# Moving LayerNorm's row factor from the matmul input to the residual add, and reordering the first batch, in a fused attention and MLP kernel

**Chip and metric.** One core of one Trainium2 chip. The metric is device time in microseconds (us). The time before is 672.65 us (median of three runs, 672.63 to 672.81). Spans below are the first to the last instruction of one profiled execution, some 2 us shorter than the device time.

## The reference

Eight batches; attention with normalized queries and keys, then LayerNorm and an MLP with a residual. Cut to what matters:

```python
# q, k, v: (8, 12, 448, 64) float32
q_n, k_n = rmsnorm(q, g_q), rmsnorm(k, g_k)
attn = softmax(q_n @ k_n^T / 8)
x = (attn @ v) -> (8, 448, 768)
mu, var = mean(x), mean((x - mu) ** 2)           # per row
xn = (x - mu) / sqrt(var + 1e-6) * g_ln
out = x + relu(xn @ w_ch1) @ w_ch2               # 768 -> 3072 -> 768
```

The row factor rs = 1/sqrt(var + eps) is positive, so relu(rs * a) = rs * relu(a): it can be left out of `xn` and applied to the row of the MLP's result. This identity is what the change uses.

## The kernel before

TensorE (PE) does all matmuls and transposes. Twelve heads make six pairs a batch; one pair has seven scores (matmul and exponential) and seven value steps. While the MLP of batch b runs on PE, the scores and values of batch b + 1 are slipped between its chunks. Batch 0 has nothing to hide behind, so its attention runs alone at the start. A batch has three row tiles of 128 (384 tokens); every second batch has a fourth tile, made of the leftover 64 tokens of two batches. The parts that matter, cut:

```python
def load_unit(self, u):                 # a unit: one or two pairs; K, Q, V
    ...
    for n, src in ((1, self.k), (0, self.q), (2, self.v)):
        eng.dma_start(<384 rows>)
        for e in range(2):
            eng.dma_start(<64 leftover rows>)

# PSUM accumulators of the values: one pair of buffers for all pairs
c["oA"] = self.ps_o.tile([128, 3, 130], FP32, tag="oA")
c["oB"] = self.ps_o.tile([128, 130], FP32, tag="oB")

def root():                                        # LayerNorm of a batch
    for t in range(n):
        nc.vector.bn_aggr(out=mv[:, t], in_=st[:, t, 0:18])
    _rsqrt(nc, c["rs"], mv[:, 0:n, 1], ...)        # exponential on ACT, 7 DVE ops
    nc.vector.scalar_tensor_tensor(out=c["sh"], ...)         # -mean * rs
def norm(t):
    nc.scalar.activation(out=t32, in_=tiles[t], func=AFT.Identity,
                         scale=c["rs"][:, t:t + 1], bias=c["sh"][:, t:t + 1])
    nc.vector.tensor_tensor(out=c["xn", t], in0=t32, in1=sh.gln, op=ALU.mult)

def down(t, g, s):                                 # second MLP matmul
    ...
    nc.vector.tensor_tensor(out=x[:, ts(g, 384)], in0=ps[:, 0:384],
                            in1=x[:, ts(g, 384)], op=ALU.add)

def run(self):
    ...
    frac = 0.77           # the next batch's attention ends at 77% of the MLP
    upto(int(min(goal, start + (goal - start) * done / total / frac)))
```

PE, ACT, GpSimd (POOL) and the load queue (SP) run in program order; VectorE (DVE) is ordered by a scheduler.

## Time and profile before

| | us |
|---|---|
| device time | 672.65 |
| span of the profile | 670.2 |
| first MLP matmul | 67.09 |
| from one batch's first MLP matmul to the next's | 77.38, 83.20, 69.83, 83.20, 70.12, 83.21, 66.33 |
| from the last batch's to the end | 69.84 |

Add the last two rows to 67.09 and the span is there. Batches 1, 3, 5 and 7 have four row tiles, so the rows of 83.2 and 69.8 differ by their MLP's size. The first LayerNorm in the timeline of the kernel before (start, length, engine, line, operation; at the end how long the engine had been idle, and for whom):

```profile
59.02 0.16 DVE L393 SCALAR_TENSOR_TENSOR sh<-stat,rs 128x3 f32<-128x3 f32 x1
59.21 1.95 ACT L399 ACTIVATE t<-x,sh,rs 128x768 f32<-128x768 f32 x2 [1.42 <-DVE sh L393]
60.27 1.88 DVE L401 TENSOR_TENSOR xn<-t,gln 128x768 f16<-128x768 f32 x2 [1.09 <-ACT t L399]
61.29 1.74 PE L421 MATMUL psX<-id,xn 128*128 128x128 f16 x12 [6.62 <-DVE xn L401]
...
67.09 0.80 PE L436 MATMUL psH<-xnT,w 128*128 128x384 f16 x2 [1.18 <-DVE xnT L423]
```

The values ended at 54.67 us (the prediction's 54.57 is the end of the last oA matmuls, a tenth before the last oB); PE then idles 6.6 us for the first normalized tile and starts the MLP 12.4 us after the values. The second view is PE alone in a four-tile batch, with attention slipped between the MLP's chunks:

```profile
158.08 0.54 PE L220 MATMUL psS<-qT,kT 128*128 128x448 f16 x2
...
158.71 1.46 PE L436 MATMUL psH<-xnT,w 128*128 128x512 f16 x6
...
160.29 0.35 PE L220 MATMUL psS<-qT,kT 128*128 128x448 f16 x1
```

Two scores stand back to back at 158.08: a "doubled step", where the spread of 0.77 puts two attention steps behind one MLP chunk. From the first of the six MLP matmuls behind it, 158.71, to the next score, 160.29, there are 1.58 us, where six such matmuls take 1.29: PE stood still for 0.29 us.

### The profile page before, as it was taken

Reading aid. Unit: us, or ns where it says so; the run is one execution under the profiler, and the core shown is the slowest. Engines: PE = TensorE matmul, PEld = TensorE weight load, DVE = VectorE, ACT = ScalarE, POOL = GpSimd, SP = SyncE. Lnnn points to the kernel's source line nnn. Section 1 sums busy time; section 2 is a strip of 40 time slices with the busy share of each in tenths; the row PEclk is TensorE's granted clock in tenths of the full one; section 3 lists DMA queues with packets and bytes.
Section 4 is the critical chain, followed back from the end, with each engine's and each line's share of the span. In section 5 each row is a group of like instructions: output and inputs, shape, how many; then the busy total and the mean of one; then the engine's idle time right before and its main releaser. Section 6 shows DMA issues by size and latency. Waiting matters only on the chain.

```text
span 670.2 us, 12546 instructions
## 1 busy us (share of the span) xinstructions
PE 620.5 (93%) x5066; PEld 379.5 (57%) x5066; DVE 373.8 (56%) x886; ACT 384.3 (57%) x669; POOL 91.6 (14%) x115
## 2 busy tenths in 40 slices
PE   1683899999999999999999999999999999999995
PEld 1352566655566666655566666655556666654463
DVE  4867667865556466765466466774465653380010
ACT  3884687647853487647763388637764287324300
POOL 2622222201220112202220022202201020000000
PEclk9995999999999999999999999999999999999999
DMA  5999973132131342122221242203331000010011
GB/s 147 219 220 220 215 184 82 54 108 77 52 84 47 93 113 66 51 66 67 82 83 48 60 122 59 80 24 107 83 84 47 28 22 1 25 48 1 0 48 51
DMA packets 72016, 54.81 MB, mean 82 GB/s; under 512 B 22928, under 2 KB 65936, under 8 KB 71952
## 3 DMA queue, kind: packets, MB, share of 16 engines
q1 hardware_dynamic: 62704, 44.22, 23.2%
q0 software_dynamic: 8528, 9.44, 8.2%
q8 instruction: 41, 0.67, 0.4%
q10 hardware_dynamic: 720, 0.30, 0.2%
q14 instruction: 23, 0.19, 0.1%
HBM read 52.36 MB, written 11.01 MB: 95 GB/s over the span
## 4 chain that ended last, share of the span: by engine, by line
PE 79%; DVE 10%; ACT 5%; issue 2%; SPq 1%; DMA 1%; POOL 0%; DVEq 0%
PE psH L436 30%; PE psC L447 27%; PE psS L220 7%; PE oA L246 4%; PE tr L202 2%; PE tr L189 2%; ACT E L227 2%; ACT khl L155 2%; PE oB L248 2%; DVE xn L401 1%; PE psS L223 1%; PE psS L224 1%; PE psX L421 1%; DVE stat L374 1%; ACT t L399 1%
## 5 line engine op out<-in xcount | busy, mean ns | idle before, releaser
L436 PE MATMUL psH<-xnT,w 128*128 128x512 f16 (+1 forms) x1152 | 246.6, 354 | 1.5 <-DVE xnT L423 1.5
L227 ACT ACTIVATE E<-psS,rr_all 128x448 f16<-128x448 f32 x336 | 208.4, 633 | 67.8 <-PE psS L220 51.4
L447 PE MATMUL psC<-w,hT 128*128 128x384 f16 x1344 | 239.3, 326 | 0.0
L438 ACT ACTIVATE hT<-psH 128x384 f16<-128x384 f32 (+1 forms) x192 | 104.6, 545 | 119.4 <-PE psH L436 117.5
L447 PEld LDWEIGHTS <-hT 128*128 128x128 f16 x1344 | 125.4, 98 | 72.4
L436 PEld LDWEIGHTS <-w 128*128 128x128 f16 x1152 | 105.6, 98 | 84.0 <-issue 4.0
L220 PE MATMUL psS<-qT,kT 128*128 128x448 f16 x288 | 101.7, 360 | 9.8 <-ACT E L227 7.5
L150 POOL TENSOR_TENSOR t<-t,gprod 128x896 f32<-128x896 f32 x22 | 45.8, 2082 | 427.2 <-issue 199.6
L246 PEld LDWEIGHTS <-E 128*128 128x128 f16 x1008 | 72.7, 99 | 54.2 <-issue 6.6
L246 PE MATMUL oA<-v,E 128*128 128x65 f16 x864 | 68.6, 195 | 1.5 <-DVE x L263 1.5
L451 DVE TENSOR_TENSOR x<-psC,x 128x384 f32<-128x384 f32 x48 | 26.7, 555 | 60.6 <-PE psC L447 60.2
L191 DVE COPY kT<-tr 128x960 f16<-128x960 f16 x48 | 31.5, 655 | 40.1 <-PE tr L189 39.6
L248 PE MATMUL oB<-v,E 128*128 128x65 f16 x288 | 52.9, 195 | 0.2
L261 DVE RECIPROCAL rec_all<-oA 128x6 f32<-128x6 f32 x48 | 9.4, 196 | 73.8 <-PE oA L246 73.8
L207 DVE COPY qT<-tr 128x896 f16<-128x896 f16 x45 | 28.0, 622 | 29.9 <-PE tr L202 29.6
L220 PEld LDWEIGHTS <-kT 128*128 128x128 f16 x288 | 28.5, 100 | 22.5 <-issue 3.3
L158 DVE TENSOR_TENSOR khl<-t,khl 128x896 f16<-128x896 f32 x22 | 24.0, 1091 | 18.0 <-ACT khl L155 17.8
L248 PEld LDWEIGHTS <-E 128*128 128x128 f16 x336 | 32.8, 98 | 0.9 <-DVE xl L268 0.5
L144 DVE TENSOR_REDUCE ssq<-qn 128x14 f32<-128x896 f32 (+1 forms) x25 | 26.2, 1046 | 10.1 <-ACT qn L141 9.1
L401 DVE TENSOR_TENSOR xn<-t,gln 128x768 f16<-128x768 f32 x28 | 26.9, 968 | 8.8 <-ACT t L399 8.8
L144 DVE TENSOR_REDUCE ssq<-khl 128x14 f32<-128x896 f32 (+1 forms) x25 | 26.2, 1047 | 10.0 <-ACT khl L141 9.4
L399 ACT ACTIVATE t<-x,sh,rs 128x768 f32<-128x768 f32 x24 | 23.8, 1021 | 13.0 <-DVE sh L393 12.3
(83 smaller groups left out, 536.7 us busy)
## 6 DMA issues: line engine op xcount, KB each, us to landing
out_dram<-x SPq DMA_DIRECT2D x24, 384.0 KB, 2.3
t<-in_k_dram SPq DMA_DIRECT2D x22, 384.0 KB, 3.5
t<-in_q_dram SPq DMA_DIRECT2D x22, 384.0 KB, 4.1
t<-in_v_dram SPq DMA_DIRECT2D x22, 384.0 KB, 4.3
w<-in_moe_w_ch_dram POOLq DMA_DIRECT2D x3, 1536.0 KB, 24.1
w<-in_moe_w_ch_dram POOLq DMA_DIRECT2D x2, 2304.0 KB, 44.1
out_dram<-xl SPq DMA_DIRECT2D x8, 192.0 KB, 3.1
t<-in_k_dram SPq DMA_DIRECT2D x44, 32.0 KB, 3.5
```

What stands on the lines that cost most here:

```text
L144: nc.vector.tensor_reduce(out=c["ssq"][:, n], in_=c["sq", n], axis=AX.X, op=ALU.add)
L150: nc.gpsimd.tensor_tensor(out=c["t"][:, 1], in0=c["t"][:, 1], in1=sh.gprod.unsqueeze(1).broadcast_to([128, g, D]), op=ALU.mult)
L191: nc.vector.tensor_copy(out=kT.rearrange("p g d -> p (g d)"), in_=ps[:, 0:960])
L220: nc.tensor.matmul(ps[:, 0:S], kT[:, 192 + 128 * i:320 + 128 * i], qT[:, h * S:(h + 1) * S], start=True, stop=True)
L227: nc.scalar.activation(out=c["E"][:, i], in_=ps[:, 0:S], func=AFT.Exp, scale=self.rr[:, 1, g:g + 1], bias=EXP_BIAS)
L246: nc.tensor.matmul(oA[:, t, cs], E[:, i, ts(t, 128)], rhs, start=(i == 0 and t == 0), stop=(i == 6 and t == 2))
L248: nc.tensor.matmul(oB[:, cs], E[:, i, 320:448], rhs, start=(i == 0), stop=(i == 6))
L399: nc.scalar.activation(out=t32, in_=tiles[t], func=AFT.Identity, scale=c["rs"][:, t:t + 1], bias=c["sh"][:, t:t + 1])
L401: nc.vector.tensor_tensor(out=c["xn", t], in0=t32, in1=sh.gln, op=ALU.mult)
L436: nc.tensor.matmul(ps[:, 0:N], sh.w1[:, dc, ts(f, 128)], xnT[:, dc, 0:N], start=(dc == 0), stop=(dc == NDC - 1))
L438: nc.scalar.activation(out=hT[:, f, 0:N], in_=ps[:, 0:N], func=AFT.Relu)
L447: nc.tensor.matmul(ps[:, 0:384], hT[:, f, ts(t, 128)], sh.w2[:, f, ts(g, 384)], start=(f == 0), stop=(f == NFF - 1))
```

## The change

Its intent: (1) leave rs out of the normalized tile, so that LayerNorm needs one DVE pass per tile instead of an ACT and a DVE pass, and no root ahead of it; (2) load the first batch tensor by tensor and order its preparation by hand; (3) a second pair of value accumulators in batch 0, in the MLP's PSUM buffers, which are idle then; (4) spread the attention over the MLP until ten chunks of 0.96 us before its end, instead of 77%. XS = 32 is multiplied into LayerNorm's weight and taken out again in the row factor. The core of the diff (cut: loads, checks of rs's range, small preparation ops):

```diff
+FIRST_ORDER = [      # (step, unit, operations of that unit's preparation)
+    (-2, 0, "begin", "sq", "sk", "kg", "tq", "rootq", "tk", "khi", "qn", "qdup", "klo", "rootk"),
+    (-2, 1, "begin", "sk", "sq", "kg", "tk", "tq", "khi"),
+    (-1, 1, "root", "klo", "qn", "qdup"),
+    ...
+]
+XS = 32.0
@@ loads of batch 0
+        for eng, n in ((nc.sync, 0), (nc.scalar, 1)):    # Q, K
+            main(eng, n, 0)                              # pair 0
+            left(eng, n)                                 # leftovers of all 12 heads
+        main(nc.scalar, 1, 1)
+        ...
+            nc.sync.dma_start(sh.gln, ...)
+            nc.vector.tensor_scalar(out=sh.gln, in0=sh.gln, scalar1=XS, ...)
@@ values
+            if p in (1, 3, 5):
+                c["oA"] = self.ps_m.tile([128, 3, 130], FP32, tag="mlp", name="oA")
+                c["oB"] = self.ps_m.tile([128, 130], FP32, tag="mlp", name="oB")
@@ LayerNorm
-            nc.scalar.activation(out=t32, in_=tiles[t], func=AFT.Identity,
-                                 scale=c["rs"][:, t:t + 1], bias=c["sh"][:, t:t + 1])
-            nc.vector.tensor_tensor(out=c["xn", t], in0=t32, in1=sh.gln, op=ALU.mult)
+            nc.vector.scalar_tensor_tensor(out=c["xn", t], in0=tiles[t], scalar=mv[:, t, 0:1],
+                                           in1=sh.gln, op0=ALU.subtract, op1=ALU.mult)
         def first():
+            aggregate()
+            for t in range(3):
+                norm(t)
             root()
-            norm(0)
-            norm(1)
@@ copies of the transposes, first batch
+        if b == 0 and t < 2:
+            nc.scalar.copy(out=self.xnT[:, :, ts(t, 128)], in_=ps)
@@ residual
-                nc.vector.tensor_tensor(out=x[...], in0=ps[:, 0:384], in1=x[...], op=ALU.add)
+                nc.vector.scalar_tensor_tensor(
+                    out=x[...], in0=ps[:, 0:384], scalar=self.rs[:, b, t:t + 1],
+                    in1=x[...], op0=ALU.mult, op1=ALU.add)
@@ run
-            upto(self.pos + 2)
-        frac = 0.77
+            upto(self.pos + 1)
+        tail = 10
-                upto(int(min(goal, start + (goal - start) * done / total / frac)))
+                upto(int(min(goal, start + (goal - start) * done / (total - 960 * tail))))
```

## The prediction

> **What bounds the kernel now.** I read the page's totals and slices first, then the chain of waits, then who TensorE (PE) waited for, stretch by stretch.
>
> ```profile
> span 670.2 us, 12546 instructions
> PE 620.5 (93%) x5066; PEld 379.5 (57%) x5066; DVE 373.8 (56%) x886; ACT 384.3 (57%) x669; POOL 91.6 (14%) x115
> PE   1683899999999999999999999999999999999995
> PE 79%; DVE 10%; ACT 5%; issue 2%; SPq 1%; DMA 1%; POOL 0%; DVEq 0%
> ```
>
> PE is full from about the fifth of 40 slices (16.8 us each) to the last. A busy PE need not be at its peak, so I checked the rate in the chain in order of time:
>
> ```profile
> 67.09 4.39 PE psH L436 x18
> ...
> 144.63 1.29 PE psH L436 x6
> ...
> 297.66 1.29 PE psH L436 x6
> ...
> 631.83 31.21 PE psC L447 x192
> ```
>
> Six matmuls of 512 columns take 1.29 us, 215 ns each; 192 of 384 columns take 31.21 us, 163 ns each. Two batches take 297.66 - 144.63 = 153.0 us; the next two pairs of batches, read the same way, 153.3 and 153.5. So from the first MLP at 67.09 to the last matmul at 663.04 the kernel is 596 us of PE work with little air, and the change takes no matmul away: both compiled kernels have 11,915 instructions on PE, in the listings of each engine’s order that can be had without running them; the order of the changed one is read there too. What is left to win is before 67.09 and in the idle time between. In a table of stretches (columns: length, then PE, weight loads, DVE, ACT and POOL busy us with counts, granted clock, DMA share, GB/s):
>
> ```profile
> 0.00:15.00 15.00, 2.33 (x16) 1.69 (x17) 6.22 (x23) 4.76 (x9) 3.25 (x11) 1.00 0.54 141
> 15.00:30.00 15.00, 9.24 (x66) 5.25 (x64) 12.69 (x27) 11.65 (x21) 10.12 (x14) 1.00 0.87 216
> 30.00:45.00 15.00, 10.85 (x133) 7.22 (x133) 11.06 (x29) 13.67 (x24) 6.61 (x7) 1.00 1.12 220
> 45.00:60.00 15.00, 7.62 (x92) 4.93 (x88) 8.68 (x31) 7.25 (x13) 0.00 (x0) 0.76 1.16 220
> 60.00:67.00 7.00, 2.46 (x18) 1.78 (x19) 6.70 (x10) 4.93 (x7) 4.10 (x4) 0.50 1.25 219
> 67.00:109.00 42.00, 39.93 (x343) 25.41 (x343) 28.89 (x63) 32.88 (x63) 10.19 (x12) 0.97 0.89 180
> ```
>
> PE is busy for 32.5 of the first 67 us. From 15 to 30 DVE is the fullest, from 30 to about 52 ACT (13.67 of 15), then comes a serial stretch of LayerNorm. PE's waits, whole run and first 67 us:
>
> ```profile
> PE psX L421 <- DVE xn L401: 10.7, 6, 6.6
> PE tr L186 <- DVE khl L158: 10.1, 1, 10.1
> PE psS L220 <- ACT E L227: 7.5, 17, 2.1
> ...
> PE psX L421 <- DVE xn L401: 8.7, 2, 6.6
> ```
>
> Of the 10.7 us that PE waited for the normalized tile, 8.7 lie in the first LayerNorm and only 2.0 at all later ones, 0.5 at a time. That is the size of what the LayerNorm part can give later.
>
> **What the skill says.** "TensorE: Matmul & The Clock Gate", section "Back-to-back issue gap": N/2.4 + 2.5 ns between matmuls when warm, N/1.2 when cold. The trace agrees: 215 ns at 512 warm, 0.32 us between the first matmuls of 384 at 67.09, 0.163 later. Its section "What's actually happening" says that about 3.4 us of activity release the clock; here the weight loads after 67.09 keep the cold spacing until 69.61. "VectorE: DVE Perf Modes", section "The perf-mode tier table": an fp32 tensor_tensor runs one element a cycle and cannot go faster. It has no row for the fused three-operand form; the trace has both on 128x896 at 1091 ns (tensor_tensor) and 1092 ns (fused), so I price fused as tensor_tensor. "DMA: Bandwidth & Descriptors", section "Specifications", gives 512 B as the least transfer for line rate; the leftover rows go in pieces of 256 B, and the change puts those of all 12 heads first. No row of this trace isolates that.
>
> **The change, part by part, in the first stage.**
>
> *Start.* Before, issue was slow: SP needs about 0.6 us an issue, 9 issues a unit, and the batch's last load went out at 22 us. After, Q and K of pair 0 come with the leftovers of all heads (six times the pieces), so I put their landing at 7.2 instead of 5.97 (K). From there I walked the changed order of each engine by hand with durations of the trace: square 0.58, reduce 0.62, small DVE operation 0.2, K product on POOL 1.13, low half 0.62, copy of K transposed 0.65, qn 0.63. K's transposes start at 10.7 (before 10.12). But DVE's new order puts the reductions of pair 1 ahead of pair 0's last root step and qn, so qn ends at 14.2, its duplicate (now on DVE) at 14.8, the transposes at 15.9, the copy of qT at 16.7, and the first exponential starts at 17.2 (before 16.84). Nothing is won here; pair 1 and the squares of the third unit are further along.
>
> *Pair 0 to pair 1.* ACT has two exponentials done at 18.3, then its order wants the root of unit 2, whose DVE work ends at 20.6. Three more exponentials, then the copy of pair 1's qT, which needs qn of pair 1, and that stands in DVE's queue behind the scaling of the LayerNorm weight, which needs a load issued behind the whole batch (about 23 us at the 220 GB/s that the table shows). That gives seven exponentials done at 27.3; before, nine were done at 26.98.
>
> *The ACT-bound stretch.* In the old kernel, 33 exponentials from 26.98 at 0.61 us, plus squares and high half of unit 3 (3 x 0.95), a root (0.22) and two qT copies (2 x 0.91), make 25.0 and end at 52.0; the trace has 51.99, so the sum is a fair model. After: 35 exponentials at 0.59 (second pair of accumulators), 2 x 0.95 since the high half moves to POOL, 0.22 and 1.82, from 27.3: 51.9. So the move of three high halves (0.57 + 2 x 0.95 = 2.5 us of ACT) and the earlier squares are eaten by the slower start.
>
> *Last pair.* In the old kernel PE waited 1.03 us for the accumulator of pair 4 to be read, then ran all of pair 5's value matmuls: 2.6 us from last exponential to the end. With accumulators in the MLP's PSUM for pairs 1, 3 and 5 they keep up: 0.4 us, ending at 52.3 instead of 54.57.
>
> *First LayerNorm.* Before: 67.09 - 54.57 = 12.5 us (evacuation, statistics, aggregate 2.8; root 1.85; two passes per tile on ACT and DVE; third tile behind squares of the next batch). After, from the end of the values: aggregate done at 2.8, three fused passes of 0.94 end at 5.6, with no root ahead of them; then ACT has the root's exponential (6.0), a square of 0.95 (7.0) and two copies of transposes at about 0.8: 8.55. Saved 3.95. So the first MLP matmul moves from 67.1 to 52.3 + 8.55 = 60.9: 6.2 us.
>
> *Later.* ACT loses 28 passes of 1.02 us and DVE keeps 28 passes of the same length (0.97); neither bounds. The residual add, 0.555 us, becomes a fused form of equal price. What goes is the 2.0 us of waits at the boundaries: first tile ready about 4.3 us after the last accumulator instead of 7.5. The shorter tail (ten chunks of 0.96 us instead of 10.6 and 14.1 us) still covers that. The root is needed only by the first residual, tens of us later.
>
> *Sum.* 6.2 + 2.0 = 8.2. My walk charged every stall that DVE's order permits and kept the whole cold start of the MLP (8 matmuls at 0.32 instead of 0.163, 1.25 us); I take 1.2 us of that back as likely too harsh. 672.65 - 9.4 = 663.2.
>
> **Rivals.** (1) The start is better than my walk: pair 0's scores at 12 to 13 us because Q and K land at 6 and DVE does not wait for pair 1. For: the author ordered this by hand, surely for that; ACT has spare time before 25 us. Against: DVE's printed order. It would add up to 4 us: 657 to 660, and some of it is over 2%. (2) Transfers take over: the table shows 216 to 220 GB/s without a break to about 90 us, the first 15 us at 141. An MLP that starts 6 us earlier wants its weights and the next batch earlier. For: the queue was full. Against: all of the batch goes out sooner, the second MLP weight had landed at 92 and was first used at 108.5. If it bites, 2 to 4 us come back: 666. (3) PE's own work is the limit and the later stages give nothing, or the denser spread of the attention makes ACT late: 665 to 667. (4) DVE gets longer queues at the boundaries (three passes in a row) and delays K and Q copies of the next pairs: 0.5 us each, 3 in all.
>
> **Range and chances.** The front is uncertain by 3.5 us either way, the later stages by 2, so 656.5 to 668.5. Over 2% means under 659.2, a win of 13.5 us of the 34.6 that PE idled in the first 67: 0.22. Slower by over 2% has no mechanism I can find, 0.02. Within 2%: 0.76.
>
> **What would show it.** First MLP matmul near 60.9 (58 to 63.5); first exponential near 17; ACT the fullest from 27 to 52; end of the values to first MLP matmul 8.5 us; no wait of PE on the normalized tile after the first batch; 153 us for two batches unchanged; the last 31 us unchanged. I would be wrong if the two-batch time moves by over 1 us, if the first exponential comes before 14.5, or if PE waits for weights after the first MLP starts.

## The result, and the profile after

662.25 us (median of four runs, 661.82 to 662.91) against 672.64 us (four runs, 672.23 to 672.81). The ratio is 0.9847, 95% interval 0.983 to 0.9864: 1.5% less, in the class "same" at the 2% line. The span of the profile went from 670.2 to 660.8 us.

From the page of the changed kernel: span, totals, and the chain of waits by engine.

```profile
span 660.8 us, 12501 instructions
PE 618.4 (94%) x5066; PEld 380.7 (58%) x5066; DVE 377.6 (57%) x890; ACT 358.4 (54%) x641; POOL 92.5 (14%) x113
PE 83%; DVE 8%; ACT 4%; DMA 2%; issue 1%; SPq 1%; ACTq 0%; DVEq 0%
```

ACT lost 26 us of work, DVE gained 4, PE kept its 5066 matmuls. Nearly all of ACT's 26 us was beside PE's work, as the small gain says. The chain in order of time, about the first MLP matmul of batches 0, 1 and 3:

```profile
61.08 7.28 PE psH L523 x30
...
138.00 1.29 PE psH L523 x6
...
290.07 1.29 PE psH L523 x6
```

The rate of the matmuls is the same (1.29 us for six), the first MLP starts 6.01 us earlier, and two batches take 290.07 - 138.00 = 152.07 us instead of 153.03. The table of stretches of the changed kernel (length, then PE, weight loads, DVE, ACT and POOL busy us with counts, granted clock, DMA share, GB/s):

```profile
0.00:15.00 15.00, 0.93 (x7) 0.66 (x7) 8.87 (x32) 4.24 (x10) 3.52 (x9) 1.00 0.80 226
15.00:30.00 15.00, 9.31 (x54) 5.25 (x55) 11.82 (x28) 10.24 (x17) 10.86 (x11) 1.00 0.96 243
30.00:45.00 15.00, 12.39 (x155) 8.78 (x154) 12.36 (x31) 12.98 (x24) 7.13 (x10) 1.00 1.12 213
45.00:60.00 15.00, 8.93 (x110) 6.04 (x106) 10.45 (x30) 8.38 (x15) 0.22 (x1) 0.85 1.21 221
```

The first 15 us move 226 GB/s instead of 141, yet PE does less there (0.93 us instead of 2.33): the earlier data does not reach PE. ACT remains the fullest between 30 and 45. PE's waits over the whole run (who waited for whom: us in total, times, longest):

```profile
PE tr L262 <- DVE khl L218: 11.3, 1, 11.3
PE psS L296 <- ACT E L302: 5.7, 11, 2.3
...
PE psX L505 <- DVE xn L479: 4.0, 1, 4.0
...
PE psC L534 <- DVE x L538: 1.9, 4, 0.5
```

The wait for the normalized tile is 4.0 us, all of it in the first LayerNorm; before it was 10.7, six times. A new one is the last line: four times 0.5 us, PE waits for a residual add to free an MLP buffer. There is no wait for weights. The first LayerNorm in the timeline:

```profile
55.62 2.81 DVE L479 SCALAR_TENSOR_TENSOR xn<-x,stat,gln 128x768 f16<-128x768 f32 x3
56.63 2.68 PE L505 MATMUL psX<-id,xn 128*128 128x128 f16 x18 [4.04 <-DVE xn L479]
58.69 0.95 ACT L198 ACTIVATE khl<-qkv 128x896 f32<-128x896 f32 x1
59.55 1.48 ACT L508 COPY xnT<-psX 128x768 f16<-128x768 f16 x2
59.78 2.07 POOL L207 TENSOR_TENSOR qkv<-qkv,gprod 128x896 f32<-128x896 f32 x1 [16.83 <-issue]
59.82 2.05 DVE L59 SCALAR_TENSOR_TENSOR stat<-stat 128x3 f32<-128x3 f32 x1
61.08 1.44 PE L523 MATMUL psH<-xnT,w 128*128 128x384 f16 x4 [1.77 <-ACT xnT L508]
```

Three fused passes, the transposes behind each, a square for the next batch, two copies, the MLP. From the end of the values (52.59) to the MLP there are 8.49 us. Note the DVE operation on 128x3 at 59.82: such ones take 0.17 us elsewhere, this one 2.05, and it ends with the POOL product beside it. Last, PE in a four-tile batch:

```profile
151.45 0.35 PE L296 MATMUL psS<-qT,kT 128*128 128x448 f16 x1
151.64 1.46 PE L523 MATMUL psH<-xnT,w 128*128 128x512 f16 x6
152.93 0.35 PE L296 MATMUL psS<-qT,kT 128*128 128x448 f16 x1
```

One score per step, and 1.29 us from the first of six matmuls to the next score: no idle time. In this kernel no four-tile batch has a doubled step; in batch 0 scores still stand back to back in three places.

**Where the 9.4 us of span came from**, by the table of batches:

| | before | after | saved |
|---|---|---|---|
| first MLP matmul | 67.09 | 61.08 | 6.01 |
| batch 0 | 77.38 | 76.76 | 0.62 |
| four-tile batches 1, 3, 5 | 83.20, 83.20, 83.21 | 82.79, 82.80, 82.79 | 0.41 each |
| three-tile batches 2, 4 | 69.83, 70.12 | 69.28, 69.27 | 0.55, 0.85 |
| batch 6 | 66.33 | 66.19 | 0.14 |
| batch 7, to the end | 69.84 | 69.84 | 0.00 |

So 6.0 before the first MLP and 3.4 after it.

### The profile page after: what moved, and what is told of

Same layout as the page of the kernel before. It is cut to its first block, busy times and chain, and to the rows that moved or that the text cites. A ratio compares the mean times of both kernels' runs of the same rounds, so it can differ in the third digit from the quotient of the medians. Undisturbed runs are those within 1.5% of the kernel's fastest.

```text
span 660.8 us, 12501 instructions
## 1 busy us (share of the span) xinstructions
PE 618.4 (94%) x5066; PEld 380.7 (58%) x5066; DVE 377.6 (57%) x890; ACT 358.4 (54%) x641; POOL 92.5 (14%) x113
## 4 chain that ended last, share of the span: by engine, by line
PE 83%; DVE 8%; ACT 4%; DMA 2%; issue 1%; SPq 1%; ACTq 0%; DVEq 0%
PE psH L523 31%; PE psC L534 30%; PE psS L296 7%; PE oA L325 4%; PE tr L278 2%; PE tr L265 2%; DVE xn L479 2%; ACT E L302 2%; PE oB L327 1%; PE psS L299 1%; PE psS L300 1%; PE psX L505 1%; DVE stat L459 1%; DMA hT<-in_k_dram 1%; DVE kT L267 1%
## 5 line engine op out<-in xcount | busy, mean ns | idle before, releaser
L207 POOL TENSOR_TENSOR qkv<-qkv,gprod 128x896 f32<-128x896 f32 x21 | 43.8, 2084 | 418.2 <-issue 301.8
L538 DVE SCALAR_TENSOR_TENSOR x<-psC,rs_all,x 128x384 f32<-128x384 f32 x48 | 29.5, 616 | 74.8 <-PE psC L534 74.4
L327 PE MATMUL oB<-v,E 128*128 128x65 f16 x288 | 52.3, 194 | 0.0
L218 DVE TENSOR_TENSOR khl<-qkv,khl 128x896 f16<-128x896 f32 x21 | 22.9, 1093 | 16.4 <-ACT khl L215 16.2
L54 ACT ACTIVATE stat<-stat 128x3 f32<-128x3 int32 (+1 forms) x8 | 1.7, 209 | 50.8 <-DVE stat L53 50.8
L342 DVE TENSOR_TENSOR x<-oA,rec_all 128x384 f32<-128x384 f32 x48 | 26.8, 558 | 1.5
```

The source lines that it names most:

```text
L207: nc.gpsimd.tensor_tensor(out=c["t"][1], in0=c["t"][1], in1=sh.gprod.unsqueeze(1).broadcast_to([128, g, D]), op=ALU.mult)
L327: nc.tensor.matmul(oB[:, cs], E[:, i, 320:448], rhs, start=(i == 0), stop=(i == 6))
L538: nc.vector.scalar_tensor_tensor(out=x[:, ts(g, 384)], in0=ps[:, 0:384], scalar=self.rs[:, b, t:t + 1], in1=x[:, ts(g, 384)], op0=ALU.mult ...
```

## The experiments

Each kernel was timed in three rounds beside the kernel before on the same chip (four runs of each new kernel). Its baseline's medians were 671.99, 671.80 and 671.92 us in the three series. The intervals are wide enough (0.2% either way) that I read parts of a microsecond from the traces, not from the times.

A trace is one execution, and scatters too. The changed kernel and four of its variants below (old spread, plain add, both versions of copies first) have the same code up to the end of the values; in their traces the first exponential starts between 17.35 and 17.63 us and the values end between 52.49 and 52.75. And the profiled execution need not be a typical one: in the second experiment it was the fastest of four (672.33, median 673.99).

One thing differs by chance between traces. At the start of the first MLP the matmuls of 384 columns run at half the clock for a while ("cold", 0.32 us apart instead of 0.16). The same code up to there gave 14 cold matmuls in the changed kernel (granted clock 0.50 from 61.1 to 65.6 us, 1.00 from 65.7) and 10 with the old spread (0.50 to 64.3, 1.00 from 64.4). So up to about 0.7 us of batch 0's length (an estimate from these spacings) is no property of the kernel.

**Theories at the start.** A: the parts add: about 4 us from LayerNorm and 2 from the accumulators in the first stage, and the later 3.4 from the vanished waits on LayerNorm. C, its rival: much of the later 3.4 comes from the new spread. I also held that the hand-made order and the loads give about nothing.

### LayerNorm part alone, in the kernel before

Edit: the kernel before, with the LayerNorm, copies, residual and scaling hunks of the diff; old loads, old order, one accumulator pair, `frac = 0.77`.

> The kernel before with the LayerNorm part alone (row deviation in the residual add, three fused passes on VectorE, two of the first three transposed tiles copied by ScalarE); loads, order of the first batch, accumulators and spread as before. Theory A (the LayerNorm part gives the 4 us of the first LayerNorm and also the 3.4 us that the later batches won): values of pair 5 still end near 54.6, first MLP matmul at about 63 (before 67.1), each later batch 0.4 to 0.8 us shorter, time 665 to 666. Theory B (the order of the loads and of the first batch carries most): 669 to 671. Theory C (the shorter tail carries the later gain): first MLP matmul at 63 but batches as long as before, 668 to 669.

Measured: 668.98 us, ratio 0.9956 (0.9934 to 0.9978), span 666.7. First MLP at 64.14 (values end at 55.25, so LayerNorm took 8.9 instead of 12.4); batches 78.42, 83.22, 69.32, 83.20, 69.32, 83.21, 65.99. PE's waits on the normalized tile are no longer listed after the first LayerNorm, and the three-tile batches come to 69.32 as in the changed kernel. The four-tile batches do not move at all, and batch 0 gets 1.0 us longer. The cold stretch covers that: 16 cold matmuls here and 8 in the kernel before, 1.1 us by their spacings (an estimate). Theory A expected too much.

### Everything but the LayerNorm part

Edit: the changed kernel with the old LayerNorm:

```diff
-            nc.vector.scalar_tensor_tensor(out=c["xn", t], in0=tiles[t], scalar=mv[:, t, 0:1],
-                                           in1=sh.gln, op0=ALU.subtract, op1=ALU.mult)
+            nc.scalar.activation(out=t32, in_=tiles[t], func=AFT.Identity, ...)
+            nc.vector.tensor_tensor(out=c["xn", t], in0=t32, in1=sh.gln, op=ALU.mult)
  (root, copies and residual as before)
```

> The changed kernel with the old LayerNorm and the old residual add; loads, order of the first batch, accumulators and the tail of ten chunks as changed. Theory A: values of pair 5 end at 52.3, first MLP matmul 12.5 us later at about 64.8, later batches as long as in the kernel before (383.3 us from the second batch's MLP to the sixth's), time about 670.2. Theory B: first MLP matmul by 62, time 667 or less. Theory C (the tail gives the later gain): first MLP matmul at 64.8 but the later batches 3 us shorter in sum, time about 667.

Measured: 673.99 us, ratio 1.0035 (1.0018 to 1.0052), span 670.6: slower than the kernel before, by 2.3 us of time (1.2 to 3.5), though the trace, of the fastest execution of four, shows only 0.4. The first MLP starts at 64.66, 2.4 us earlier, but all of that is lost later: three-tile batches 70.58, batch 6 67.4. PE's waits from 80 us on:

```profile
PE psX L505 <- DVE xn L485: 7.8, 7, 1.7
```

Before, that wait was 2.0 us in the same stretch. The tail of ten chunks is too short to hide the old LayerNorm (root, then two passes per tile), one boundary after another. So the parts do not add: LayerNorm alone gives 3.5 us of span (3.0 by the ratio of the times), the rest alone costs 0.4 (2.3), both together give 9.4 (10.3).

### The old spread in the changed kernel

```diff
-        tail = 10
+        frac = 0.77
-                upto(int(min(goal, start + (goal - start) * done / (total - 960 * tail))))
+                upto(int(min(goal, start + (goal - start) * done / total / frac)))
```

> The changed kernel with the old spread of the attention over the MLP (0.77 of the work instead of all but ten chunks). Theory A (the spread hardly matters): 662.0 to 662.8, batch lengths within 0.2 us of the changed kernel's. Theory C (the spread gives the later gain): about 665, batches 0.4 to 0.8 us longer.

Measured: 665.31 us, ratio 0.9903 (0.9887 to 0.992), span 662.9. First MLP at 61.24; batches 77.54, 83.21, 69.32, 83.21, 69.32, 83.21, 65.98. Of the 2.1 us of span that it loses, 0.78 are in batch 0 and 0.42, 0.41 and 0.42 in the four-tile batches; batch 6 wins 0.21 back. Theory C holds: the spread carries 1.9 of the later 3.4 us. The other 1.5 is what is left for the LayerNorm part, which gave 1.6 us in batches 2, 4 and 6 of the first experiment. (This trace had 10 cold matmuls against 14, so the spread's share is rather larger, about 2.6 by the same estimate.) The 0.41 goes with the doubled step shown above: the kernel before has it, the changed one has not, and with the old spread it is back (two scores in a row at 152.39) and the 0.41 too. The spacing of PE's matmuls accounts for all of it: in batch 1, with either kernel of the old spread, 0.29 us are lost at the score behind the doubled step and 0.13 at a later transpose of Q; in the changed kernel neither. The trace of the kernel before shows what ended both: the code has two score buffers, the exponential that read the first of the two scores ended at 160.24 and the next score started at 160.29; the copy of K's transposes ended at 186.32 and Q's transposes started at 186.37. I did not test it with more buffers. In the three-tile batches the two spreads come out even (69.28 and 69.32): the new one saves 0.42 us at a score and 0.30 at a normalized tile, and pays 0.64 at a residual add.

### One accumulator pair in the changed kernel

```diff
-            if p in (1, 3, 5):
+            if False:
```

> The changed kernel with one pair of accumulators for all pairs of the first batch, as before. Mine: the values of pair 5 wait for pair 4's evacuation and run cold after it, 2.2 us at the end and about 0.6 us of small waits earlier, so first MLP matmul near 63.5 and time about 664.7. Rival: only the recorded wait of 1.0 us counts, 663.3.

Measured: 666.03 us, ratio 0.9916 (0.99 to 0.9933), span 663.2. Values end at 55.11 instead of 52.59, first MLP at 63.21 instead of 61.08. The wait for an accumulator, which the prediction found in the kernel before and the second pair removed, is back:

```profile
PE oA L325 <- DVE x L342: 3.1, 3, 1.9
```

So the second accumulator pair is worth 2.1 us before the first MLP. The batches from the second on do not move. The kernel with everything but the LayerNorm part started its MLP 2.4 us earlier than the kernel before; take these 2.1 us off, and 0.3 us remain for loads and hand-made order: about nothing, and no more than the scatter of traces.

By the times the old spread and the single accumulator pair cost more than their traces show: 3.8 and 4.6 us by the ratios (0.9903 and 0.9916 against 0.9847), 2.1 and 2.4 by the spans. The changed kernel was not timed again beside them; its trace is of its second slowest execution, and that of the single pair of its fastest. What else is in the difference is not known.

### A plain residual add (wrong)

```diff
-                nc.vector.scalar_tensor_tensor(out=x[...], in0=ps, scalar=rs, in1=x[...], MULT, ADD)
+                nc.vector.tensor_tensor(out=x[...], in0=ps, in1=x[...], op=ALU.add)
```

This leaves the row factor out; the result is wrong (relative error 0.417).

> The changed kernel with the old plain add as its residual (wrong result on purpose: the row deviation is left out). The changed profile shows the fused add at 616 ns against 555 and PE waiting 1.9 us in four boundaries for it. If the fused form costs on the path: 660.3, the four waits gone. If the four waits come from the three normalizing passes that stand before the add in VectorE's queue, they stay and the time is 662.0 to 662.4.

Measured: 662.37 us, ratio 0.9859 (0.984 to 0.9878), span 660.8, the same as the changed kernel, and PE still waits 1.7 us for residual adds (1.9 with the fused form). The fused add is longer (616 ns instead of 555) but not on the path. The new waits on it do not come from its length; the three LayerNorm passes that now stand together in DVE's queue remain as the likely cause. They are not the whole of it: with the same passes and the old spread (the third experiment), and with the short tail and the old LayerNorm (the second), no such wait is listed.

### The copies of the first LayerNorm ahead of the next batch's preparation

In the timeline of the changed kernel ACT's square (58.69) stands ahead of the two copies that PE waits for. The edit starts the next batch's preparation after the copies; in the first version three steps of it then pass, in the second four, so that later steps are as even as in the changed kernel.

```diff
-        for op in self.ln_ops(0):
+        for x, op in enumerate(self.ln_ops(0)):
             op()
-            upto(self.pos + 1)
+            if x > 1:
+                upto(self.pos + 2 if x == 2 else self.pos + 1)    # second version: self.pos + 2
```

> The changed kernel with the first step of the next batch's preparation (a square of 0.95 us on ScalarE, the product on GpSimd) emitted after the third transposed tile instead of ahead of the first. The changed profile has that square end at 59.6 and the two copies of xnT after it, the last at 61.03. Mine: first MLP matmul at about 60.1, 0.95 us earlier, time 661.3. Rival: VectorE's copy or the root ends then, and it stays at 61: 662.2.

Measured, first version: 663.84 us, ratio 0.9882 (0.9864 to 0.99), span 662.0. The first MLP did come 0.8 us earlier (60.27), but batch 0 took 78.73 instead of 76.76. PE's waits show why:

```profile
PE tr L275 <- DVE kT L267: 6.1, 7, 1.4
```

In the changed kernel this wait was 3.3 us in four places; here it is 6.1 in seven. One step fewer ahead of the MLP shifted where batch 0's steps double up (scores back to back in four places instead of three), and PE now waits up to 1.4 us for a copy of K's transposes.

> e6 mended: there my edit let only three steps of the next batch pass before the first MLP instead of four, so that later steps came in pairs and PE waited 1.4 us for a K copy and 0.9 for scores. Here again four steps pass, all after the first two transposed tiles. If doubled steps made e6's first batch 2 us longer: first MLP matmul at 60.3 as in e6, first batch about 76.8 (e6: 78.7), time 661.3. If it was the later preparation itself: the first batch stays near 78.7, time 663.5.

Measured, second version: 662.18 us, ratio 0.9857 (0.9841 to 0.9874), span 660.3. First MLP at 60.09, batch 0 at 77.22; the wait on K's copy is back at 3.3 us. One step more gives back 1.5 of the 2.0 us. What is left of the idea is 0.5 us of span, which the times do not show (662.18 and 662.25; ratios 0.9857 and 0.9847).

### DVE's order by hand at the start

The prediction put the late first exponential down to DVE's queue (reductions of pair 1 ahead of pair 0's Q). This kernel orders the first 15 steps of DVE by hand as well, pair 0 first, and moves the scaling of the LayerNorm weight to POOL at a later step:

```diff
-    (-2, 0, "begin", "sq", "sk", "kg", "tq", "rootq", "tk", "khi", "qn", "qdup", "klo", "rootk"),
-    (-2, 1, "begin", "sk", "sq", "kg", "tk", "tq", "khi"),
+    (-3, 0, "begin", "sq", "sk", "kg", "tq", "tk", "root", "khi"),
+    (-3, 1, "begin", "sk", "sq", "kg"),
+    (-3, 0, "klo", "qn", "qdup"),
     ...
+        with self.tc.manual_schedule(engines={ENG.DVE}):
+            upto(15)
```

> The changed kernel with VectorE also held to emission order in the first 15 steps, pair 0's two roots joined, pair 1's reductions behind pair 0's qn, the scaling of the LayerNorm weight on GpSimd at step 22. Mine (VectorE's order is what made the start no faster than before): first exponential at about 15.6 instead of 17.4, values of pair 5 end near 49.5 instead of 52.6, first MLP matmul near 58, time 659. Rival (loads or ScalarE bound the start): first exponential after 17, time 662 or more.

Measured: 664.13 us, ratio 0.9889 (0.9873 to 0.9906), span 661.4. A miss: the first exponential started at 17.81 (17.42 in the changed kernel). The values did end 1.4 us earlier (51.23), but the MLP started at 62.13, a microsecond later. Timeline of this kernel's first LayerNorm:

```profile
54.91 5.25 DVE L483 SCALAR_TENSOR_TENSOR xn<-x,stat,gln 128x768 f16<-128x768 f32 x3
55.76 2.09 POOL L208 TENSOR_TENSOR qkv<-qkv,gprod 128x896 f32<-128x896 f32 x1 [11.26 <-ACT khl L199]
```

The same three passes took 2.81 us in the changed kernel. Here the product of the next batch falls into them, and they take 5.25: the first still takes 1.01, the second ends at 58.67, 0.8 us after the product (57.85), the third at 60.16, 0.8 us after the copy of V that follows on POOL (59.35). That POOL's operations hold them up is my reading of these times; the next kernels vary it.

### All three edits together

DVE's order by hand and copies first, as above, and the second K load on SP's queue instead of ACT's:

```diff
-        main(nc.scalar, 1, 1)
-        for n, p in ((0, 1), (2, 0), (2, 1)):
+        for n, p in ((1, 1), (0, 1), (2, 0), (2, 1)):
             main(nc.sync, n, p)
```

First with three steps behind the copies, then with four.

> e7 and e6 together, and pair 1's K load issued by SyncE so that ScalarE's table load does not stand behind a wait for an earlier load (it started at 5.72 in the changed kernel). Mine: first square at about 6.5 instead of 7.13, first MLP matmul near 56.7, time 657.5 to 658.5. Rival (Q and K of pair 0 land only at 7): as e7 less 0.9.

Measured, with three steps: 662.54 us, ratio 0.9863 (0.9847 to 0.988), span 660.5, well short of what was expected. With the copies first the product no longer meets the three passes, which take 2.87 us, and the MLP starts at 59.35; batch 0 loses it again by doubled steps (78.18). At the start of this kernel stands this pair:

```profile
15.49 2.08 POOL L207 TENSOR_TENSOR hT<-hT,gprod 128x896 f32<-128x896 f32 x1
15.85 1.76 DVE L52 TENSOR_SCALAR ssq<-ssq 128x14 f32<-128x14 f32 x1
```

An operation of 14 columns takes 1.76 us, to within 0.04 us of the product's end. ACT's part of pair 1's root waits for it (17.64) and stands ahead of the exponentials in ACT's order, so the first of these starts only at 17.75.

> e8 with that same mending, everything else as e8. First MLP matmul at 59.4, first batch about 76.8 instead of 78.2, time about 660.7 if doubled steps are the cause; 662.5 if not.

Measured, with four steps: 661.21 us, ratio 0.9845 (0.9828 to 0.9861), span 659.2: first MLP 59.73, batch 0 76.56.

### The first products on DVE itself

The same, with K's products of units 0 to 2 on DVE instead of POOL (their place in the order moves with them):

```diff
-            nc.gpsimd.tensor_tensor(out=c["t"][1], in0=c["t"][1], ...)
+            (nc.vector if u < 3 else nc.gpsimd).tensor_tensor(out=c["t"][1], in0=c["t"][1], ...)
```

> e10 with the K products of units 0 to 2 on VectorE (0.6, 0.6 and 1.1 us) instead of GpSimd (1.13, 1.13 and 2.08). In the traces small VectorE operations end when a GpSimd product ends (1.76 us for one of 0.18 in e8 at 15.85, 5.25 us for three passes of 0.95 in e7 with a product beside them, 2.87 in e8 without). If GpSimd's product holds VectorE up: first exponential at about 16.4 instead of 17.75, first MLP matmul near 58, time 659.5, although VectorE has 2.3 us more to do. If it does not, the added work shows: first exponential 18 or later, time 661.5 or more.

Measured: 660.57 us (660.11 to 661.45), ratio 0.9836 (0.9819 to 0.9852), span 658.3; first MLP at 59.18, where 58 was expected. The first exponential starts at 16.51, 1.2 us earlier than in the run before this one, though DVE has about 2.3 us more to do (an estimate: two products at 0.61 us, which the trace shows, and one of twice the size):

```profile
15.80 0.52 DVE L52 TENSOR_SCALAR ssq<-ssq 128x14 f32<-128x14 f32 x1
...
16.51 1.89 ACT L302 ACTIVATE E<-psS,rr_all 128x448 f16<-128x448 f32 x3
```

This is the fastest kernel found by the median. Its span is 2.5 us under that of the changed kernel, but its trace is of the fastest of four executions; by the times the medians differ by 1.7 us and the intervals overlap (0.9836 and 0.9847), so that it is faster than the changed kernel is not shown. Since the order moved with the product, this run shows that the two together are worth 1.2 us at the first exponential, and the length of the 14-column operation (1.76, now 0.52, where it ends 0.03 us after a cast on POOL) speaks for the product.

## Why the prediction was right, and where its steps were not

The time (662.25 against 663.2 predicted) and the class were right. The sum 6.2 + 2.0 + 1.2 = 9.4 equals the span saved, but two of its three terms were wrong and cancelled: 2.0 and 1.2 were predicted, 3.4 and none measured. That the total was met so closely is luck.

| step of the prediction | predicted | measured |
|---|---|---|
| first exponential | 17.2 | 17.42 |
| last exponential ends | 51.9 | 52.08 |
| values end | 52.3 | 52.59 |
| end of the values to first MLP matmul | 8.55 | 8.49 |
| first MLP matmul | 60.9 | 61.08 |
| gain in the first stage | 6.2 | 6.01 |
| gain later | 2.0 | 3.4 |
| "taken back as too harsh" | 1.2 | none |

**The front: right.** The walk of each engine's order gave the milestones of the table to 0.3 us. The two carriers are shown by experiment: the accumulators (2.1 us; the prediction had 2.6 - 0.4 = 2.2) and the first LayerNorm (3.9 between the two traces; without it the MLP starts 3.6 us later although the values end 0.7 us earlier, so 4.3 by that run). That the hand-made order and loads win nothing was right as well. One reason was incomplete: the walk had only DVE's order, and its misses partly cancelled (K's transposes start at 11.30 against 10.7 predicted, but the copy of qT is done at 16.79 against 16.7). The chip has a second one that it did not see, POOL's products holding up DVE's small operations. DVE's order by hand alone did not move the first exponential forward (17.81); with the products moved off POOL as well it came at 16.51. "SBUF — State Buffer" in the Trainium skill, section "SBUF: two separate sides", says that VectorE and GpSimd share a pair of ports which is locked for a whole instruction, so that the loser blocks, if VectorE's operation has two SBUF inputs or runs in a mode that uses two ports; the traces agree (0.17 us become 2.05 beside a product of 2.07; 2.81 become 5.25; a copy from PSUM beside a product keeps its 0.62).

**"I take 1.2 us of that back": wrong.** It was a hedge against the walk, and the walk was right: 60.9 against 61.08. Even the part about the clock went the other way. The prediction kept 8 cold matmuls at the start of the MLP; 14 had the cold spacing (weight loads 0.32 us apart until 65.52, from 61.08), some 0.9 us more (an estimate from the spacings). This number is not fixed by the kernel: the one with the old spread, the same code up to there, had 10.

**"What goes is the 2.0 us of waits": mis-sized.** The waits did go, and that was worth about 1.5 us on the path (what the old spread leaves of the later gain). The other 1.9 us came from the spread, which the prediction had only as a cost to be covered ("the shorter tail still covers that") and, in its third rival, as a danger. The direction was the reverse: the denser attention is the more even one, with no doubled step in a four-tile batch. "153 us for two batches unchanged" did not hold: the two later pairs read above went from 153.03 and 153.33 to 152.07, by 0.96 and 1.26 us, the second over the limit of 1 us that the prediction set itself. (Its third pair, 153.5, is a misreading: the last batch starts at 600.36, not at 604.52, so the pair took 149.4.)

**"A fused form of equal price": wrong, without effect.** 616 ns instead of 555; the equal price held between operands in SBUF (1092 and 1091) and did not carry over to a PSUM operand. The plain add shows that the difference is off the path.

**The rivals.** The better start (1) fell: 17.42. Transfers (2): they moved 226 instead of 141 GB/s in the first 15 us, and PE never waited for weights. "Nothing later" (3) fell by the table of batches. Longer DVE queues at the boundaries (4) exist, as four waits of 0.5 us on residual adds, but the batches that have them are shorter than before all the same.

**What the prediction did not ask: do the parts add?** They do not. The short tail is a gain only with the short LayerNorm: with the old one batches 2, 4 and 6 are 0.8, 0.5 and 1.1 us longer than with the old spread (70.59, 70.58 and 67.40 against 69.83, 70.12 and 66.33).

**Left open.** What the 256-byte leftover pieces cost at the start. What sets the number of cold matmuls in an execution. Why the times of two experiments show a larger loss than their traces.

## What to carry to other kernels

When a factor can be moved from the input of a matmul to its output, count what it frees on the path at the boundaries, not the engine time: here taking 26 us off ACT and the root off the boundary gave 3.5 us by itself. When two streams share one engine, look at how evenly one is slipped into the other: doubled steps cost from 0.4 us a batch up to a single wait of 1.4 us, and one step more or fewer at the start can make or undo them. And test the parts of a change apart and together: a shorter tail that loses beside a long LayerNorm can win once the chain that it must hide is shorter.

## What the Trainium skill lacked or had wrong

- "VectorE: DVE Perf Modes", the perf-mode tier table, has no row for the fused three-operand form: 1092 ns on 128x896 from SBUF, as tensor_tensor (1091); but 616 ns on 128x384 with a PSUM operand, where tensor_tensor takes 555.
- "SBUF — State Buffer" has the rule for the shared port pair of VectorE and GpSimd, but no times of a compute operation held up by it: one of 0.17 us took 2.05 beside a product of 2.07 us, one of 14 columns 1.76 beside 2.08, and three passes of 2.81 us took 5.25.
- No page says what it costs to put two steps of a secondary stream behind one chunk of the main one: 0.42 us a batch here (0.29 at a score, 0.13 at a transpose), and single waits of up to 1.4 us for a copy of K's transposes.
